# Head 0's row maxima through a scaled unit matrix, and a reordered prologue, in a bucketed-attention plus two-MoE kernel

## The chip, the cores and the metric

The kernel runs on one core of a Trainium2 chip. The metric is the device time of one execution in microseconds (us), the median of several runs. The engines are TensorE (PE in the profile; PEld is its weight load), VectorE (DVE), ScalarE (ACT), GpSimd (POOL) and SyncE (SP), which here only issues transfers. A q behind a name (SPq, ACTq) marks the instructions of an engine's sequencer, transfers above all. Each engine executes its own instructions in the order in which the program gives them.

## What is computed

Attention over 16 heads (batch 2 x 8), 768 positions, head size 64, in which a query sees only the keys of its own hash bucket, followed by two feed-forward layers (left out below, the change doesn't touch them):

```
q_bits = (einsum('bhsd,dk->bhsk', q, proj) > 0);  k_bits likewise      # 6 bits
mask   = q_bucket[..., :, None] == k_bucket[..., None, :]
scores = where(mask, q @ k^T / 8, -1e9)
attn   = exp(scores - max(scores)) ;  attn /= sum(attn) + 1e-9
out    = attn @ v                    # then moe(out), then moe2(...)
```

A row without any key in its bucket gets the plain mean of v.

## The kernel before

The heads go two at a time: a pair p holds heads 2p and 2p+1, on 64 partitions each. For a pair, `split_k`, `split_q` and `low_q` cut k and q into a rounded high part and a rest (`kH`, `kL`, `qH`, `qL`, in the fp32r format). For pair 0 VectorE makes the rests, for pair 1 GpSimd does, from values that ScalarE rounds or scales first. `bits` multiplies them with the projection (`prH`, `prL`, made from `pr` in `setup`) in six matmuls for each half of 384 positions, and a comparison on VectorE turns the sums into plus or minus one half (`bits_cmp` for head 0, `bits_bt` into the tile `bt` for the others, which `bits_out` copies by DMA into rows 64 to 75 of the head's tiles).

Each head h has a tile `KA` and a tile `QA` (in the trace both are called T, with a buffer number in the order listing: T_86 and T_91 are head 0, T_87 and T_92 head 1, and so on): rows 0 to 63 hold the high part, rows 64 to 75 the bits. `KB` and `QB` hold what the rounding left. Rows 96 and 97 of `QA` hold the row's maximum in two parts, and the same rows of `KA` are -1, so that the score matmul subtracts the maximum itself.

The work of a head:

- `max_unit(h, qt)`, six of them: for 128 queries, two matmuls (line 614) against all keys, and two VectorE reductions (line 618) to the maximum. Three PSUM buffers ("m") are shared by these and by the bit products.
- `max_fin` and `max_out`: the maxima (`mq`) are transposed on TensorE (line 634), split in two on VectorE (lines 637 and 638, tile `mr`) with a flag for rows without keys (`mf`, line 643), and copied by two DMAs into rows 96 and 97 of `QA`, by a third into `FL`. For head 0 this is done for each half of the queries.
- `scores(h, hf, i)`, six units s = 6h + 3hf + i: for 256 keys by 384 queries, two matmuls of 128 rows (KB, QB) and two of 98 rows (KA, QA), line 664. Then `Exp` on ScalarE twice (`E`, line 668, and rounded to fp16, `ph`, line 671), and on GpSimd the rest `pl` (line 686). Two PSUM buffers ("s") hold the scores; the prologue's bit products of pair 0 use the same two.
- `pv(h, hf, q)`: 20 matmuls (lines 698 to 704) with `ph`, `pl`, the flags and v, six units behind the scores (LAG = 6).

The order is written out by hand. `prologue()` loads pair 0, makes head 0's bits and maxima and, between the maxima, filler matmuls (`warm`, line 742) that write nothing that is used. Then a loop over the units s issues `pv(s-6)`, `scores(s)`, the maxima of later heads, and the tasks that tables put at unit s: `at(s, ...)` before, `po(s, ...)` at the end of the unit. Up to s = 7 the tasks stand behind the scores and the maxima of their unit. The maxima of head 1 are taken at s = 0 (one `max_unit`), 1 (one) and 2 (four). Constants such as E2 and E4 say at which s pair 1's row copies (`asm_k`, `asm_q`), `bits` and `bits_out` stand.

## Time and profile before

| | us |
|---|---|
| median of 3 runs | 680.44 |
| the three runs | 680.24, 680.44, 682.21 |
| the profiled execution | 680.07 |
| its span, first to last instruction | 678.3 |

| engine | busy, us | share of the span |
|---|---|---|
| PE | 662.5 | 98% |
| PEld | 611.0 | 90% |
| DVE | 510.2 | 75% |
| ACT | 432.5 | 64% |
| POOL | 338.2 | 50% |

Matmuls overlap and their ends are modelled, so a PE busy share of 98% says that it seldom had nothing in flight; it is the gaps, and what it did between them, that have to be read from the timeline. A timeline row gives the start, the length, the engine, the line, what was written and read, how many instructions the row merges, and, in brackets, how long the engine was idle before and what ended that. For a row of two matmuls the length covers both.

### The profile page before, as it was taken

The page shows a single profiled execution, that of the slowest core. Times are in us where ns is not written, and L with a number is a line of the kernel's source. Part 1 is how long each engine was busy: PE and PEld are TensorE (multiplying, and loading weights), DVE is VectorE, ACT ScalarE, POOL GpSimd, SP SyncE. Part 2 cuts the span into 40 slices and gives each one's busy share as a digit, 9 for nine tenths or more (in the row PEclk, how much of TensorE's full clock was granted, in tenths as well). Part 3 has the DMA queues.
Part 4 walks back from the last instruction along what each step waited for, and adds up shares of the span by engine and source line. Part 5 has one row for each costly group of instructions (what it writes and reads, how often), then busy time and mean ns, then how long its engine had stood idle before and what let it go on. Part 6 is the DMA issues. An engine that isn't in the chain of part 4 may idle for free.

```text
span 678.3 us, 13481 instructions
## 1 busy us (share of the span) xinstructions
PE 662.5 (98%) x5189; PEld 611.0 (90%) x5189; DVE 510.2 (75%) x978; ACT 432.5 (64%) x749; POOL 338.2 (50%) x280
## 2 busy tenths in 40 slices
PE   8999999999999999999999999999999999999998
PEld 7789998888898989999999999988989898989886
DVE  6798988999985557677768778754868787877664
ACT  6578788889888525465665657776656565565520
POOL 6688888999988240654542673122233131313100
PEclk9899999999999999999999999999999999999999
DMA  6656656767441000222114322010303121211005
GB/s 192 168 150 150 172 143 159 197 167 190 101 98 65 1 2 31 65 86 68 62 63 125 126 63 93 32 63 0 125 21 104 32 95 36 89 63 62 1 0 187
DMA packets 22527, 61.80 MB, mean 91 GB/s; under 512 B 3864, under 2 KB 4952, under 8 KB 22464
## 3 DMA queue, kind: packets, MB, share of 16 engines
q1 hardware_dynamic: 22032, 60.55, 31.3%
q8 instruction: 41, 0.67, 0.4%
q10 hardware_dynamic: 432, 0.40, 0.2%
q14 instruction: 22, 0.18, 0.1%
HBM read 38.87 MB, written 3.15 MB: 62 GB/s over the span
## 4 chain that ended last, share of the span: by engine, by line
PE 63%; DVE 6%; ACT 2%; issue 1%; POOLq 0%; DVEq 0%; ACTq 0%
PE c L1210 16%; PE m L1210 11%; PE x L1538 10%; PE m L1538 9%; PE c L147 4%; PE m L307 3%; PE m L1453 2%; PE s L664 2%; PE c L1453 2%; PE x L1210 1%; PE x L698 1%; DVE xF L1161 1%; PE x L699 1%; PE x L700 1%; DVE mx L618 1%
## 5 line engine op out<-in xcount | busy, mean ns | idle before, releaser
L686 POOL TENSOR_TENSOR pl<-E,ph 128x768 f16<-128x768 f32 x85 | 152.4, 1807 | 30.7 <-ACT ph L671 17.1
L618 DVE TENSOR_REDUCE mx<-m 128x1 f32<-128x384 f32 x192 | 96.7, 546 | 13.1 <-PE m L614 12.1
L668 ACT ACTIVATE E<-s 128x768 f32<-128x768 f32 x96 | 78.0, 813 | 38.5 <-PE s L664 31.5
L671 ACT ACTIVATE ph<-s 128x768 f16<-128x768 f32 x85 | 68.9, 811 | 0.0
L698 PEld LDWEIGHTS <-ph 128*128 128x128 f16 x576 | 53.7, 97 | 16.3 <-issue 10.2
L698 PE MATMUL x<-VV,ph 128*128 128x65 f16 x576 | 64.2, 195 | 2.8 <-DVE xo L718 1.8
L699 PE MATMUL x<-VV,ph 128*128 128x65 f16 x576 | 63.8, 195 | 0.0
L700 PE MATMUL x<-VV,pl 128*128 128x65 f16 x576 | 63.3, 192 | 0.0
L664 PE MATMUL s<-QB,KB 128*128 128x384 f32 x192 | 57.0, 378 | 0.0
L614 PE MATMUL m<-T,T 76*128 76x384 f32 x192 | 54.0, 354 | 2.7 <-DVE mx L618 1.5
L699 PEld LDWEIGHTS <-ph 128*128 128x128 f16 x576 | 54.3, 98 | 0.7 <-issue 0.6
L700 PEld LDWEIGHTS <-pl 128*128 128x128 f16 x576 | 54.5, 99 | 0.0
L664 PE MATMUL s<-T,T 98*128 98x384 f32 x192 | 49.6, 339 | 0.2 <-DMA T<-mr 0.2
L1006 POOL TENSOR_TENSOR hF<-hF 128x256 f32<-128x256 f32 x8 | 6.9, 859 | 75.5 <-DVE hF L965 75.5
L614 PEld LDWEIGHTS m<-T,T 76*128 76x128 f32 x192 | 35.2, 189 | 8.3 <-DVE mx L618 5.5
L961 DVE SCALAR_TENSOR_TENSOR wy<-wy,wr 128x512 int32<-128x512 int32 x32 | 23.0, 718 | 22.0 <-ACT wr L956 22.0
L1556 DVE TENSOR_TENSOR xF<-x,xF 128x512 f32<-128x512 f32 (+1 forms) x43 | 29.4, 684 | 11.6 <-PE x L1538 11.5
L1094 POOL TENSOR_TENSOR hF<-hF 128x256 f32<-128x256 f32 x6 | 6.5, 1091 | 62.7 <-DVE hF L1048 62.7
L984 POOL TENSOR_TENSOR wl<-wy,wh 128x512 fp32r<-128x512 f32 x10 | 13.0, 1298 | 46.4 <-ACT wh L982 46.4
L664 PEld LDWEIGHTS s<-T,T 98*128 98x128 f32 x192 | 35.2, 190 | 0.5 <-DMA T<-mr 0.5
L984 POOL TENSOR_TENSOR wol<-wy,woh 128x512 fp32r<-128x512 f32 x6 | 8.4, 1393 | 50.9 <-ACT woh L982 50.9
L1556 DVE TENSOR_TENSOR xF<-m,xF 128x512 f32<-128x512 f32 (+1 forms) x42 | 28.5, 678 | 4.6 <-PE m L1538 4.6
(472 smaller groups left out, 2185.1 us busy)
## 6 DMA issues: line engine op xcount, KB each, us to landing
wraw<-in_wts_dram SPq DMA_DIRECT2D x56, 512.0 KB
xF<-in_vP_dram SPq DMA_DIRECT2D x8, 384.0 KB
KB<-kH SPq DMA_DIRECT2D x15, 192.0 KB
QB<-qL SPq DMA_DIRECT2D x15, 192.0 KB
T<-kH SPq DMA_DIRECT2D x15, 192.0 KB
T<-qH SPq DMA_DIRECT2D x15, 192.0 KB
KB<-kL SPq DMA_DIRECT2D x15, 192.0 KB
QB<-qH SPq DMA_DIRECT2D x15, 192.0 KB
```

The lines of the kernel that those rows point to most:

```text
L614: pe.matmul(u[:, 0:HF], QA[h % NA][0:76, qt * 128:qt * 128 + 128], KA[h % NA][0:76, hsl(hf)], start=True, stop=True,)
L618: dve.tensor_reduce(out=mx[h][:, qt, hf:hf + 1], in_=u[:, 0:HF], axis=AX.X, op=ALU.max)
L664: pe.matmul(u[:, k, 0:HF], a[0:n, c], b[0:n, hsl(hf)], start=n == 128, stop=n < 128)
L668: act.activation(out=e, in_=u[:, :, 0:HF], func=AF.Exp, scale=BIG)
L671: act.activation(out=ph.rearrange("p (a b) -> p a b", a=2), in_=u[:, :, 0:HF], func=AF.Exp, scale=BIG,)
L686: eng.tensor_tensor(out=pl, in0=e, in1=ph, op=ALU.subtract)
L698: pe.matmul(o, ph[:, c], vv[:, 0:65], start=kt == 0, stop=False)
L699: pe.matmul(o, ph[:, c], vv[:, 65:130], start=False, stop=False)
L700: pe.matmul(o, pl[:, c], vv[:, 0:65], start=False, stop=False)
L1210: pe.matmul(u, l[:, s], r[i], start=first and i + j == 0, stop=i == 1 and j == 2, skip_group_check=not first,)
L1538: pe.matmul(u[:, 0:c1 - c0], (h, l, h)[k], (oh, oh, ol)[k][:, c0:c1], start=j == k == 0, stop=j == 1 and k == 2,)
L1556: dve.tensor_tensor(out=o, in0=u[:, 0:c1 - c0], in1=o, op=ALU.add)
```

## The change

Six edits, all of which act before head 1's scores:

- `load_qk(0)`: the projection `pr` is the first transfer on ScalarE's queue; before, it stood behind the first half of q.
- `prologue`: the row copies of head 0 (`own_rows`) stand behind the splits of both halves, and the four filler matmuls behind each half's bit products go (WARM 4 to 0).
- `bits_bt` of head 1 moves from ahead of the first `max_unit` to ahead of the fourth (B0 0 to 3).
- Head 0's maxima are no longer transposed and copied into `QA`. `max_diag(hf)` makes, for each half, the negated maxima, split in two (`nm`, `nh`, `nl`), and multiplies the unit matrix by them, column scale by column scale: three VectorE operations into `xh0[0]`, three ScalarE operations into `xl0[0]`. `scores` of head 0 then adds them with four more matmuls a unit, with a matrix of ones (`xh0[1]`) as weights; its second pair of matmuls reads 76 rows rather than 98.
- `max_flag(hf)` transposes the maxima for the flag alone, at s = 0 and s = 2.
- The split of pair 1 leaves the prologue for the end of unit 0, and its row copies and bit products stand at unit 1 rather than 0.

```
-B0 = 0
-F0 = 2
+B0 = 3
-WARM = (9, 4, 3, 1)
+WARM = (9, 0, 3, 1)
-E2 = (0, 0, 2)
+E2 = (1, 1, 2)
-E4 = ((0, 0), (2, 4), (3, 7))
+E4 = ((1, 1), (2, 4), (3, 7))
...
+            st["one"] = xh0[1][:, 0:128]
+            pool.memset(f32(st["one"]), 1.0)
...
+                act.dma_start(out=pr, in_=projT)
                 for c in (hsl(0), hsl(1)):
                     sp.dma_start(out=kr[:, c], in_=kT[p][:, c])
                     act.dma_start(out=qr[:, c], in_=qT[p][:, c])
-                    if c.start == 0:
-                        act.dma_start(out=pr, in_=projT)
...
+        def max_diag(hf):
+            n = a2.tile([128, 3], F32, name="nm")
+            dve.tensor_scalar(
+                out=n, in0=st["mq", 0][:, 3 * hf:3 * hf + 3], scalar1=-1.0, scalar2=0.5,
+                op0=ALU.mult, op1=ALU.min,
+            )
+            nh = a2.tile([128, 3], F32R, name="nh")
+            dve.tensor_copy(out=nh, in_=n)
+            nl = a2.tile([128, 3], F32, name="nl")
+            dve.tensor_tensor(out=nl, in0=n, in1=f32(nh), op=ALU.subtract)
+            d = [x[0][:, hsl(hf)] for x in (xh0, xl0)]
+            for b in range(3):
+                c = slice(128 * b, 128 * b + 128)
+                dve.tensor_scalar(
+                    out=d[0][:, c], in0=ident, scalar1=f32(nh)[:, b:b + 1], scalar2=None,
+                    op0=ALU.mult,
+                )
+                act.activation(
+                    out=d[1][:, c], in_=ident, func=AF.Identity, scale=nl[:, b:b + 1]
+                )
+            st["D", hf] = d
+
+        def max_flag(hf):
+            u = unit()
+            pe.transpose(u[0:3, 0:128], st["mq", 0][:, 3 * hf:3 * hf + 3], ident)
+            g = a2.tile([6, 128], F16, name="mf")[0:3]
+            dve.tensor_scalar(out=g, in0=u[0:3, 0:128], scalar1=-0.5, scalar2=None, op0=ALU.is_lt)
+            sp.dma_start(out=FL[0][0:1, hsl(hf)], in_=g)
...
-            for a, b, n in ((KB[h], QB[h], 128), (KA[h % NA], QA[h % NA], 98)):
+            for a, b, n in ((KB[h], QB[h], 128), (KA[h % NA], QA[h % NA], 98 if h else 76)):
...
+            for j in range(0 if h else 2):
+                for k in range(2):
+                    pe.matmul(
+                        u[:, k, 0:HF], st["one"], st["D", hf][j], start=False, stop=j == 1
+                    )
...
                 low_q(0, c)
+            for c in (hsl(0), hsl(1)):
                 own_rows(c)
...
-            split_k(1, slice(0, S), True)
-            split_q(1, slice(0, S), True)
-            low_q(1, slice(0, S))
...
                 warm(WARM[2] if qt < 3 else WARM[3])
-                if qt == F0:
-                    max_fin(0, 0)
-                    max_out(0, 0)
+                if qt % 3 == 2:
+                    max_diag(qt // 3)
...
+            if p == 1:
+                po(0, split_k, 1, slice(0, S), True)
+                po(0, split_q, 1, slice(0, S), True)
+                po(0, low_q, 1, slice(0, S))
...
-                po(E3[0], max_fin, 0, 1)
-                po(E3[1], max_out, 0, 1)
+                for i in range(2):
+                    po(E3[i], max_flag, i)
```

How the order moves, at three places. Line numbers of the changed kernel differ (scores 694 and 699, `Exp` 703 and 706, bit products 146, filler 777).

VectorE, from the comparison for head 1's bits (`bt`) to head 0's last maxima, before:

```order
L513 TENSOR_SCALAR bt<-s,pr 128x384 x2
L618 TENSOR_REDUCE mx<-m 128x1 x6
L625 TENSOR_REDUCE mq<-mx 128x3
L637 TENSOR_SCALAR mr<-m 3x128
L638 SCALAR_TENSOR_TENSOR mr<-m,mr 3x128
L643 TENSOR_SCALAR mf<-m 3x128
```

and after, from the first of head 0's reductions:

```order
L618 TENSOR_REDUCE mx<-m 128x1 x6
L625 TENSOR_REDUCE mq<-mx 128x3
L649 TENSOR_SCALAR nm<-mq 128x3
L654 CAST nh<-nm 128x3
L656 TENSOR_TENSOR nl<-nm,nh 128x3
L660 TENSOR_SCALAR xh_97<-ident,nh 128x128 x3
L513 TENSOR_SCALAR bt<-s,pr 128x384 x2
```

The `bt` comparisons moved behind the first half's maxima, and six new operations took the place of three; in both kernels six more reductions follow, and after those, in the changed one, the six operations again.

ScalarE, from the last of the constants (T_95) to the second score unit, before:

```order
L410 ACTIVATE T_95<-pr 32x768
L442 ACTIVATE kH<-kr 128x768
L457 ACTIVATE qH<-qr 128x768
L463 ACTIVATE qr<-qr 128x768
L668 ACTIVATE E<-s 128x768
```

and after (xl_101 is the tile `xl0[0]`):

```order
L411 ACTIVATE T_95<-pr 32x768
L664 ACTIVATE xl_101<-ident,nl 128x128 x6
L703 ACTIVATE E<-s 128x768
L706 ACTIVATE ph<-s 128x768
L442 ACTIVATE kH<-kr 128x768
L457 ACTIVATE qH<-qr 128x768
L463 ACTIVATE qr<-qr 128x768
```

The six scalings of both halves now stand ahead of the first `Exp`, and the three split operations of pair 1 between the first unit's `Exp` and the second's.

TensorE, from the first score unit to pair 1's bit products, before (head 1's first maxima between them):

```order
L664 MATMUL s<-QB,KB 128x384 x2
L664 MATMUL s<-T_91,T_86 128x384 x2
L614 MATMUL m<-T_87,T_92 128x384 x2
L147 MATMUL m<-kH,prH 128x384
L147 MATMUL m<-qH,prH 128x384
```

and after, from the second score unit on:

```order
L694 MATMUL s<-QB,KB 128x384 x2
L694 MATMUL s<-T_91,T_86 128x384 x2
L699 MATMUL s<-xh_97,xh_98 128x384 x2
L699 MATMUL s<-xl_101,xh_98 128x384 x2
L614 MATMUL m<-T_87,T_92 128x384 x2
L543 MATMUL m<-vs_s,ones 128x1
L146 MATMUL m<-kH,prH 128x384
L146 MATMUL m<-qH,prH 128x384
```

The twelve bit products (two of them shown) now stand between the second and the third score unit rather than between the first and the second, and a score unit has eight matmuls rather than four.

## Rows read from the trace of the kernel before

**Rows 1.** Busy time and granted clock in three stretches, columns as the first line says

```profile
core 0: us, PE busy (x) PEld busy (x) DVE busy (x) ACT busy (x) POOL busy (x), PEclk, DMA share, GB/s
27.00:31.00 4.00, 3.98 (x15) 3.38 (x15) 2.60 (x7) 1.62 (x2) 2.27 (x2) 0.57 0.77 163
36.00:50.00 14.00, 13.54 (x173) 12.20 (x172) 12.83 (x35) 10.48 (x14) 11.10 (x7) 1.00 0.66 159
100.00:245.00 145.00, 140.14 (x1895) 126.59 (x1894) 122.29 (x282) 115.28 (x170) 120.34 (x76) 1.00 0.47 119
```

**Rows 2.** Timeline of the prologue (start us, length us), splits and bits of pair 0

```profile
0.99 4.21 PE L742 MATMUL x<-ones 128*128 128x128 f32 x18 [0.99 <-POOL ones L383]
...
4.30 0.51 ACT L457 ACTIVATE qH<-qr 128x384 fp32r<-128x384 f32 x1
...
4.89 0.17 DVE L379 CAST prH<-pr 64x24 fp32r<-64x24 f32 x1 [4.89 <-DMA pr<-in_projT_dram]
...
5.67 0.66 PE L147 MATMUL s<-kH,prH 128*128 128x384 f32 x1 [0.48 <-ACT T L479]
5.77 0.56 DVE L443 TENSOR_TENSOR kL<-kr,kH 128x384 fp32r<-128x384 f32 x1
...
6.13 0.52 PE L147 MATMUL s<-qH,prH 128*128 128x384 f32 x1
...
6.45 0.52 PE L147 MATMUL s<-kH,prL 128*128 128x384 f32 x1
...
7.40 1.05 PE L742 MATMUL x<-ones 128*128 128x128 f32 x8
...
9.17 0.33 PE L147 MATMUL s<-qL,prH 128*128 128x384 f32 x1
...
9.54 1.25 DVE L513 TENSOR_SCALAR T<-s,pr 12x384 fp32r<-12x384 f32 x2 [0.52 <-PE s L147]
```

**Rows 3.** Timeline from head 0's maxima to the first Exp

```profile
15.68 1.45 SPq L142 DMA_DIRECT2D T<-mr  x2
...
16.09 2.86 DVE L618 TENSOR_REDUCE mx<-m 128x1 f32<-128x384 f32 x6
...
18.78 0.30 PEld L664 LDWEIGHTS s<-T,T 98*128 98x128 f32 x2 [0.47 <-DMA T<-mr]
...
19.44 0.81 ACT L668 ACTIVATE E<-s 128x768 f32<-128x768 f32 x1 [0.99 <-PE s L664]
```

**Rows 4.** Timeline, the split of pair 1 on ScalarE and GpSimd

```profile
15.83 0.84 ACT L442 ACTIVATE kH<-kr 128x768 fp32r<-128x768 f32 x1 [2.57 <-PE m L614]
...
16.75 1.83 POOL L443 TENSOR_TENSOR kL<-kr,kH 128x768 fp32r<-128x768 f32 x1 [1.86 <-ACT kH L442]
...
17.60 0.84 ACT L463 ACTIVATE qr<-qr 128x768 f32<-128x768 f32 x1
```

**Rows 5.** Timeline of the first units, from the first ph to the fourth scores

```profile
20.14 0.80 ACT L671 ACTIVATE ph<-s 128x768 f16<-128x768 f32 x1
...
22.70 0.60 PE L664 MATMUL s<-QB,KB 128*128 128x384 f32 x2
...
24.45 0.60 PE L664 MATMUL s<-QB,KB 128*128 128x384 f32 x2
...
25.00 0.14 DVE L549 TENSOR_SCALAR vs_t<-m 128x1 f32<-128x1 f32 x1
...
25.63 3.80 DVE L618 TENSOR_REDUCE mx<-m 128x1 f32<-128x384 f32 x8
...
30.14 0.93 PE L664 MATMUL s<-QB,KB 128*128 128x384 f32 x2
```

**Rows 6.** Timeline, SyncE's transfers to head 1's maxima, and head 1's first scores

```profile
25.92 0.66 SPq L651 DMA_DIRECT2D FL<-mf  x1
...
32.87 1.52 SPq L142 DMA_DIRECT2D T<-mr  x2
...
37.40 0.52 PE L664 MATMUL s<-T,T 98*128 98x384 f32 x2
```

More of the change, by code (lines that the diff above doesn't have):

```diff
@@ L664, in scores @@
                     pe.matmul(
-                        u[:, k, 0:HF], a[0:n, c], b[0:n, hsl(hf)], start=n == 128, stop=n < 128
+                        u[:, k, 0:HF], a[0:n, c], b[0:n, hsl(hf)], start=n == 128, stop=n == 98
+                    )
[3 more added lines that the diff above has]
+                        u[:, k, 0:HF], st["one"], st["D", hf][j], start=False, stop=j == 1
                     )
```

## The prediction, made before the changed kernel was run

> **What bounds the kernel now.** I read three views. The busy time by stretch comes first: from 100 to 245 us, most of the attention, TensorE is busy 140.14 of 145.00 us, and from 36 to 50 us 13.54 of 14.00 [rows 1]. From about 36 us on TensorE is therefore the bound, at a fixed amount of work, and a later start of that stage moves the end by the same amount, but for the idle time that it can give back: at most 0.46 + 4.86 = 5.3 us. Second, the timeline of the first 37 us, in which the stage is filled. Its marks are the first `Exp` at 19.44 us [rows 3], the second and third score units at 22.70 and 24.45, the eight reductions for head 1's maxima from 25.63, the fourth unit at 30.14 [rows 5], and head 1's first scores, which need its maxima, at 37.40 [rows 6]. Third, the timeline of SyncE's queue: the flags of head 0 leave at 25.92, head 1's maxima at 32.87, 6.95 us later, with eight other transfers between them, back to back [rows 6]. I compare the changed kernel with the last mark, 37.40 us.
>
> **The start of the prologue.** VectorE's first work waits for the projection until 4.89 us [rows 2]. Loaded first, it comes before the first rounded k and q are there; VectorE's four set-up operations then lie beside that load. TensorE, though, can't start the bits before its nine fillers end, 0.99 + 4.21 = 5.20 us, against 5.67 now: 0.47 us. The eight filler rows between the halves (four matmuls, two rows each) take 1.05 us [rows 2], of which 0.8 lie on the path to the second half's products, since these pipeline behind them. Those now end at 9.17 + 0.33 = 9.50, so then at 8.2. Head 0's four comparisons, 1.25 us for two [rows 2], end at 10.79 now; VectorE then takes them one after the other from about 7.2, so they end at 9.7. The moved `own_rows` lie on ScalarE, which has no one waiting for them before 9 us; cost nothing. The memset of the ones (128 x 128) on GpSimd lies beside its own wait; cost nothing.
>
> **Head 0's maxima.** From 9.7 us on VectorE is the chain. Six reductions take 2.86 [rows 3]. The maximum of the pairs and the three operations on 128 x 3 cost about 0.19 each (0.14 plus the hand-over, [rows 5], whose 128 x 1 operation is nearest): 0.76. The three products with the unit matrix aren't in the trace; they lie between 0.14 (128 x 1) and 0.56 (128 x 384, [rows 2]); I take 0.2, a third of the larger: 0.6. Then the two `bt` comparisons, 1.2 as those of head 0, six more reductions 2.86, and 0.76 again. Sum: 9.7 + 2.86 + 0.76 + 0.6 + 1.2 + 2.86 + 0.76 = 18.7. ScalarE's six scalings stand ahead of the first `Exp` in its queue, those of the second half too, though the first unit doesn't need these. They are unseen as well: between 0.14 and 0.51 (128 x 384, [rows 2]), I take 0.2 each, three after 18.7. First `Exp`: 19.4 us. Now it is at 19.44. The copies of the maxima by DMA, issued from 15.68, held up TensorE by 0.47 us at 18.78 [rows 3]; that wait is gone, and the new chain over VectorE and ScalarE is late in its place, at the same time. **Gain up to here: none.**
>
> **The split of pair 1.** ScalarE did it from 15.83 in idle time, and GpSimd followed from 16.75 [rows 4]. Now it stands behind the first unit's two `Exp`. From 19.4: `ph` starts 0.70 later [rows 3, 5] and takes 0.80, so `kH` starts at 20.9; the three splits start 0.885 apart (15.83 to 17.60 in two steps, [rows 4]) and end at 23.5. The second unit's `Exp` is queued behind them; it came late before as well, behind the bits, so little changes there. GpSimd's `kL` runs from 21.8 for 1.83 [rows 4], and `qL`, as long, ends at 25.5. TensorE has twelve bit products between the second unit's maxima and the third unit. It reaches them at about 22 (scores at 16.9 after the ninth reduction, second unit by 21.7), does four or five and **waits for `qL` until 25.5**. Behind the waiting product stand seven matmuls with it, then the third unit, then head 1's eight maxima, and VectorE waits for these.
>
> **The clock.** TensorE's granted clock, 1.00 elsewhere, averages 0.57 from 27 to 31 us [rows 1], that is, it is at 1.2 GHz for most of it: there TensorE did eight products at the pace of the reductions. Matmuls of 384 columns stand 0.18 apart at full clock (0.52 for a pair, 0.33 for one, [rows 6, 2]) and 0.32 apart at the lower (6.13 to 6.45, [rows 2]). In the new wait of about 3.5 us TensorE does less than in that stretch, so I take the lower clock when it resumes, until the bits are done, and the full one after. The Trainium skill (TensorE: Matmul & The Clock Gate, section on HAM oscillation) speaks against this change in the same way: bursts of matmuls with waits between them each begin at half clock. By that rule the time is the first case's below, without it that of the first rival; no row shows a wait of this length.
>
> First case: the bits end at 25.5 + 7 x 0.32 = 27.7, the third unit, eight matmuls at 0.18, at 29.2, the first product 0.35 later is with VectorE: the eight reductions begin at 29.55 instead of 25.63, **+3.9**.
>
> **The extra matmuls.** 24 in all, four in each of six units, 24 x 0.18 = 4.3 us at full clock. Those of the first three units are in the times above. Twelve remain, 2.15 us, between the eight reductions and head 1's scores, where TensorE is dense; a transposition more costs 0.2. Head 1's scores by TensorE's own work: 37.40 + 3.9 + 2.15 + 0.2 = 43.65, **+6.25**.
>
> **The flags.** The second flag now leaves VectorE only behind the eight reductions: 29.55 + 3.80 + 0.5 for the last maximum and the flag's comparison = 33.9, against 25.92. SyncE waits there, and the 6.95 us of transfers queue behind: head 1's maxima leave at 40.85. From issue to use the earlier copies took 18.78 - 15.68 = 3.1 [rows 3]; they land at 43.95, **+6.55**. This comes last, just.
>
> Sum: +6.5 us at the mark. The profiled execution took 680.07 us (its span 678.3 and 1.77 around it), so 686.6; the median of the runs shown is 0.37 higher, 680.44, and I forecast against that: **686.9 us**.
>
> **The rivals.**
>
> Full clock. TensorE doesn't slow down in the wait. Seven products take 1.25 instead of 2.25, and the reductions start at 28.55; flags, and with them head 1's maxima, come 1.0 earlier: +5.5, 686.0. For it: in the other stretches of rows 1 the clock is at 1.00. Against it: none of them holds such a wait, and 27 to 31, with a milder one, is low.
>
> Given back later. The shift at the mark is right, but VectorE, GpSimd and SyncE are not delayed as much as TensorE afterwards, and TensorE's waits for them shrink. At most 5.3 us are there [rows 1]; many are gaps of a tenth of a microsecond or two, which no lead removes. I price half: 6.5 - 2.65 = +3.85, 684.3; all of it, 681.6. Against it: SyncE and VectorE are delayed as well.
>
> Not slower: the bits find their operands. Were `qL` there when TensorE arrives, the third unit would end at 25.5 (22.0 + 12 x 0.18 + 8 x 0.18), the reductions would begin at 25.9, +0.3, and the fillers and the fourth unit, now at the lower clock (1.7 us lost from 27 to 31, [rows 1]), might run at the full one: 0.3 + 2.15 + 0.2 - 1.7 = +0.95, 681.4. It decides at `qL`'s end: 23.5 us, two earlier than I have it, so a first `Exp` by 17.4. For that the comparisons would have to end at 7.7, when the second half's bits aren't yet done. A little less still, and the kernel is faster. This is also the case in which the change does what its first half says; I think that the gain of about 1 us at 9.7 us is real and is used up by the new operations before the first `Exp`.
>
> **How the numbers follow.** Lower clock in the wait 0.45 (686.9), full clock 0.27 (686.0), given back later 0.20 (684.3), operands in time 0.08 (681.4). The lower bound: full clock and half the idle time given back, 683.2. The upper: ScalarE's scalings at 0.51 each put the first `Exp` 0.9 later, and a lower clock through the whole third unit adds 8 x 0.14 = 1.1: 688.9. Range **683.0 to 689.0**; left out are the last rival, the end of the third and what I haven't seen above, together under 2 in 10. A measurement of this kernel can tell about 0.3%, 2.0 us: slower means above 682.5. Slower 0.88; within 0.3% 0.09 (most of the last rival, and the full give-back); faster 0.03.
>
> **What would show it.** In the changed profile: VectorE's first operation before 4.4 us; head 0's comparisons done at 9.7; the first `Exp` at 19.4, led by ScalarE's scalings; ScalarE's `kH` for pair 1 at 20.9, GpSimd's `qL` ending at 25.5; TensorE idle before the sixth bit product of pair 1, at a granted clock of 0.50 afterwards; the eight reductions from 29.5; SyncE's second flag at 33.9; head 1's scores waiting for the copy of its maxima at about 44. I am wrong if the first `Exp` comes before 17.5 us, if the bits don't wait for GpSimd, or if head 1's scores shift by 6 us and the end doesn't.

## The result and the profile after

| | before | after |
|---|---|---|
| median, us (4 runs each) | 681.26 | 689.71 |
| lowest and highest | 680.24, 682.21 | 689.47, 691.09 |
| the profiled execution | 680.07 | 689.47 |
| its span | 678.3 | 687.7 |

The changed kernel takes 1.0125 times as long (95% interval 1.0111 to 1.0139): slower, as forecast, but by 8.45 us between the medians and 9.4 between the profiled executions, where I had 6.5. 689.71 lies above the range's upper end of 689.0.

Where the time went is read from the start of each unit's first `Exp`, compared unit by unit with the kernel before (units are counted from 0): 1.83 us later at unit 0, 4.76 at unit 2, 7.28 at unit 5 and 7.26 at unit 7, then 9.61 at unit 8, and 9.2 to 9.3 from unit 11 to the last of the attention, unit 95. All the loss lies in the first 53 us, in steps, and only 0.3 us of it is given back behind unit 8.

The windows of the changed kernel, in the columns of [rows 1]:

```profile
core 0: us, PE busy (x) PEld busy (x) DVE busy (x) ACT busy (x) POOL busy (x), PEclk, DMA share, GB/s
13.00:16.00 3.00, 0.11 (x1) 0.00 (x0) 2.93 (x9) 1.84 (x5) 1.11 (x2) 1.00 0.96 351
16.00:23.00 7.00, 6.51 (x24) 6.32 (x25) 5.51 (x16) 2.72 (x6) 0.00 (x0) 0.53 0.09 17
23.00:27.00 4.00, 3.55 (x21) 3.23 (x20) 1.68 (x4) 3.54 (x5) 3.41 (x2) 0.96 0.33 85
33.00:37.00 4.00, 3.98 (x17) 3.72 (x18) 1.54 (x5) 0.42 (x1) 3.20 (x2) 0.57 0.11 25
38.00:50.00 12.00, 11.64 (x126) 10.69 (x124) 9.94 (x25) 6.56 (x10) 6.59 (x4) 1.00 0.79 210
110.00:254.00 144.00, 139.10 (x1889) 125.66 (x1888) 121.30 (x280) 115.03 (x169) 119.35 (x76) 1.00 0.46 118
```

From 13 to 16 us TensorE does almost nothing (0.11 of 3.00) while VectorE is busy for 2.93; then TensorE works 16 to 23 us at a granted clock of 0.53 on average, that is at 1.2 GHz for nearly all of it. The kernel before has 1.00 there. The stage in which TensorE is the bound looks as before: 139.10 of 144 us.

The timeline of the stretch in which head 0's maxima are made and the first units start (the second `xl` and `E` are ScalarE's, start and length in us):

```profile
12.00 2.11 POOL L402 MEMSET FL<- 128x768 f16 x3
12.03 0.55 DVE L618 TENSOR_REDUCE mx<-m 128x1 f32<-128x384 f32 x1
12.80 0.63 DVE L649 TENSOR_SCALAR nm<-mq 128x3 f32<-128x3 f32 x1
13.47 0.66 DVE L654 CAST nh<-nm 128x3 fp32r<-128x3 f32 x1
14.16 0.16 DVE L656 TENSOR_TENSOR nl<-nm,nh 128x3 f32<-128x3 f32 x1
14.83 1.14 DVE L513 TENSOR_SCALAR bt<-s,pr 128x384 fp32r<-128x384 f32 x2
16.49 0.69 PE L614 MATMUL m<-T,T 76*128 76x384 f32 x1 [3.37 <-DVE mx L618]
19.21 0.17 DVE L649 TENSOR_SCALAR nm<-mq 128x3 f32<-128x3 f32 x1
19.41 0.17 DVE L654 CAST nh<-nm 128x3 fp32r<-128x3 f32 x1
19.82 0.99 ACT L664 ACTIVATE xl<-ident,nl 128x128 fp32r<-128x128 f32 x3 [4.47 <-DVE nl L656]
21.27 0.81 ACT L703 ACTIVATE E<-s 128x768 f32<-128x768 f32 x1 [0.47 <-PE s L699]
22.67 0.84 ACT L442 ACTIVATE kH<-kr 128x768 fp32r<-128x768 f32 x1
25.38 1.83 POOL L464 TENSOR_TENSOR qL<-qr,qH 128x768 fp32r<-128x768 f32 x1
25.95 0.42 PE L146 MATMUL m<-kH,prH 128*128 128x384 f32 x1 [0.45 <-DVE mx L618]
27.27 0.45 PE L146 MATMUL m<-qL,prH 128*128 128x384 f32 x1 [0.20 <-POOL qL L464]
30.38 3.81 DVE L618 TENSOR_REDUCE mx<-m 128x1 f32<-128x384 f32 x8 [0.33 <-PE m L614]
44.67 0.52 PE L694 MATMUL s<-T,T 98*128 98x384 f32 x2
```

The same `nm` and `nh` take 0.63 and 0.66 us in the first half and 0.17 each in the second. The six `xl` cost 0.33 each, between my ends. The first `Exp` [rows 3] comes at 21.27 instead of 19.44, the eight reductions [rows 5] at 30.38 instead of 25.63, head 1's first scores with the maxima [rows 6] at 44.67 instead of 37.40.

And SyncE's transfers with the one ScalarE operation that waits for them:

```profile
23.72 0.69 SPq L674 DMA_DIRECT2D FL<-mf  x1
34.61 0.69 SPq L674 DMA_DIRECT2D FL<-mf  x1
41.54 1.52 SPq L141 DMA_DIRECT2D T<-mr  x2
45.02 0.59 SPq L141 DMA_DIRECT2D KB<-kH  x1
50.75 0.85 ACT L442 ACTIVATE kH<-kr 128x768 fp32r<-128x768 f32 x1 [2.76 <-DMA KB<-kH]
52.23 0.79 ACT L703 ACTIVATE E<-s 128x768 f32<-128x768 f32 x1
```

Between 34.61 and 41.54 stand the eight other transfers of [rows 6], back to back as before. New is the last wait: the rounding of k for pair 2 overwrites the tile that `KB<-kH` reads, that copy was issued at 45.02 (36.35 in the kernel before), and ScalarE stands still for 2.76 us with the `Exp` of unit 8 queued behind. It is the step from 7.26 to 9.61. The same two rows of the kernel before:

```profile
36.35 0.59 SPq L142 DMA_DIRECT2D KB<-kH  x1
41.03 0.85 ACT L442 ACTIVATE kH<-kr 128x768 fp32r<-128x768 f32 x1 [0.30 <-DMA KB<-kH]
```

The wait grew by 2.46 us. Of these, 1.41 are the queue's: the copy left 8.67 us later, while ScalarE itself was 7.26 late. The other 1.05 are the copy's own: the wait for it ended 5.73 us after its issue, against 4.68 before. Why it took longer is open.

### The profile page after: what moved, and what is told of

The parts are those of the page before. It is cut to its first block, busy times and chain, and to the rows that moved or that the text cites. A ratio compares the mean times of both kernels' runs of the same rounds, so it can differ in the third digit from the quotient of the medians.

```text
span 687.7 us, 13503 instructions
## 1 busy us (share of the span) xinstructions
PE 668.4 (97%) x5197; PEld 616.4 (90%) x5197; DVE 514.2 (75%) x986; ACT 434.1 (63%) x755; POOL 338.5 (49%) x281
## 4 chain that ended last, share of the span: by engine, by line
PE 61%; DVE 6%; ACT 2%; issue 1%; DMA 1%; POOLq 0%; DVEq 0%; ACTq 0%; SPq 0%
PE c L1246 16%; PE m L1246 10%; PE x L1574 9%; PE m L1574 9%; PE c L146 4%; PE m L306 3%; PE m L1489 2%; PE s L694 2%; PE c L1489 2%; PE x L1246 1%; DMA wraw<-in_wts_dram 1%; PE x L733 1%; DVE xF L1197 1%; PE x L734 1%; PE x L735 1%
## 5 line engine op out<-in xcount | busy, mean ns | idle before, releaser
L694 PE MATMUL s<-T,T 98*128 98x384 f32 (+1 forms) x192 | 50.1, 342 | 0.0
L694 PEld LDWEIGHTS s<-T,T 98*128 98x128 f32 (+1 forms) x192 | 35.8, 192 | 0.0
```

The costliest lines, as they stand in the source:

```text
L694: pe.matmul(u[:, k, 0:HF], a[0:n, c], b[0:n, hsl(hf)], start=n == 128, stop=n == 98)
```

## The experiments

Times of one kernel scatter by 1.5 to 6 us, so that medians of few runs settle little; each verdict below rests on the places in the trace, and the ratio is given beside it. All are against the kernel before.

| kernel | first Exp | eight reductions from | later than before at unit 0 / 7 / 8 / 95 | ratio, 95% |
|---|---|---|---|---|
| before | 19.44 | 25.63 | 0 | 1 |
| after | 21.27 | 30.38 | 1.83 / 7.26 / 9.61 / 9.27 | 1.0125 (1.0111 to 1.0139) |
| a2_after (unedited) | 20.99 | 30.11 | 1.55 / 6.97 / 9.07 / 11.17 | 1.0115 (1.0077 to 1.0153) |
| b2_before (unedited) | 19.74 | 26.14 | 0.30 / 1.72 / 1.70 / 1.80 | one run, 681.84 us |
| e1b_flags | 21.00 | 30.11 | 1.56 / 7.37 / 8.26 / 8.55 | 1.0091 (1.0061 to 1.0120) |
| e12_flagq | 20.76 | 31.39 | 1.32 / 8.19 / 8.18 / 8.71 | 1.0087 (1.0067 to 1.0106) |
| e2_split | 21.06 | 28.30 | 1.62 / 5.04 / 7.66 / 8.80 | 1.0099 (1.0077 to 1.0121) |
| e3_fill | 20.20 | 29.25 | 0.76 / 6.02 / 7.65 / 8.47 | 1.0101 (1.0078 to 1.0123) |
| e4_split_fill | 21.72 | 27.94 | 2.28 / 4.85 / 6.11 / 6.24 | 1.0059 (1.0037 to 1.0081) |
| e5_fl | 21.13 | 30.22 | 1.69 / 8.09 / 9.27 / 9.41 | 1.0117 (1.0094 to 1.0139) |
| e13_fl2 | 19.90 | 30.52 | 0.46 / 7.33 / 10.42 / 11.57 | 1.0136 (1.0121 to 1.0151) |
| e14_comb | 21.88 | 28.09 | 2.44 / 3.38 / 3.37 / 3.63 | 1.0080 (1.0060 to 1.0101) |
| e11_nodiag | 18.36 | 27.20 | -1.08 / 2.22 / 4.91 / 4.50 | 1.0050 (1.0033 to 1.0067) |
| e7_pro | 19.05 | 27.16 | -0.39 / 1.68 / 1.68 / 1.74 | 0.9979 (0.9964 to 0.9994) |
| e16_fill | 18.23 | 24.54 | -1.21 / -0.81 / -0.82 / -0.76 | 0.9989 (0.9975 to 1.0003) |
| e17_fill2 | 18.17 | 24.40 | -1.27 / 0.57 / 1.16 / 1.26 | 1.0008 (0.9990 to 1.0027) |
| e18_fill1 | 18.36 | 25.60 | -1.08 / 2.16 / 3.61 / 4.12 | 1.0000 (0.9981 to 1.0019) |

A part of these differences is scatter. after, a2_after and e12_flagq give TensorE, VectorE and ScalarE the same instructions up to unit 3, yet head 0's first reduction begins at 9.62, 9.34 and 9.74 us, the granted clock is back at 1.00 from about 23 us in the first two and from about 20.5 in the third, and pair 1's bit products begin at 25.95, 25.68 and 24.41.

### The flags on SyncE's queue

My theory after the result: the flags hold up SyncE's queue, and the copies behind them the units from 8 on. The first edit was run twice, since the profiled execution of the first (e1_flags) took 1000.8 us and can't be compared; its other runs have the ratio 1.0085 (1.0056 to 1.0115):

```
-E3 = (0, 2)
+E3 = (3, 4)
```

> The changed kernel with head 0's two flags sent later: their transposition, comparison and copy stand at units 3 and 4 instead of 0 and 2. In the changed kernel the shift against the kernel before is 7.26 us at the Exp of unit 7 and 9.61 at unit 8, and ScalarE waits 2.76 us there for a copy of kH. Queue theory: SyncE stood still for the flags (6.0 and 3.4 us) and all copies behind came late; without that ScalarE's wait falls under 0.6 us, unit 8's shift equals unit 7's, and the time is 2.0 us less, about 687.5. Rival: the copy lands late because TensorE and ScalarE were late themselves, the queue is not the cause; then the wait stays and the time is 689.5.

> The changed kernel with head 0's two flags taken at units 3 and 4 instead of 0 and 2 (E3 = (3, 4)), so that SyncE's queue no longer waits for the flag's comparison behind the first units' maxima. The earlier kernel with this edit (0.997 of its time scaled by nothing, 688.56 median) left no usable trace; this one is for the trace. Queue theory: KB<-kH of pair 1 leaves before 41 us instead of 45.02, ScalarE's kH of pair 2 waits under 0.6 us for it instead of 2.76, the lag behind the kernel before is the same at unit 8 as at unit 7 (7.3), and the end comes 2.0 us earlier than in the changed kernel: 687.6. Rival (the jump at unit 8 is made by GpSimd or ScalarE, the copy only happens to end last): kH of pair 2 waits as long for something else, unit 8 lags by 9.2 to 9.6 as before, 689.5 within 0.5.

Inconclusive: the step at unit 8 shrank from 2.35 to 0.89, the wait of `kH` to 1.29 us. But the flags, made later, held the queue at 39.06 and 44.23, and `KB<-kH` left at 45.63, not before 41:

```profile
45.63 0.59 SPq L141 DMA_DIRECT2D KB<-kH  x1
49.39 0.85 ACT L442 ACTIVATE kH<-kr 128x768 fp32r<-128x768 f32 x1 [1.29 <-DMA KB<-kH]
```

So the copy left 0.61 later than in the changed kernel and was still done 1.36 earlier, 3.76 us after its issue: the moment of issue isn't all that counts. The next kernel keeps the flags where they are made and puts off their transfers alone (the flag's tile is called `mg` in it):

```
-            sp.dma_start(out=FL[0][0:1, hsl(hf)], in_=g)
+            st["mg", hf] = g
+
+        def flag_out(hf):
+            sp.dma_start(out=FL[0][0:1, hsl(hf)], in_=st["mg", hf])
...
                     po(E3[i], max_flag, i)
+                    po(3, flag_out, i)
```

> The changed kernel with head 0's two flags still made at units 0 and 2, but their transfers on SyncE's queue put off to the end of unit 3, behind the row copies and loads that stood behind the second flag. Queue theory (SyncE, held by the flags, sends head 1's maxima and the row copies behind them late, and ScalarE's kH of pair 2 waits for these): KB<-kL, kH and so on leave from 31 us instead of 35.4, head 1's maxima at 39 instead of 41.5, KB<-kH of unit 7 at 42.5 to 43.5 instead of 45.0, kH of pair 2 waits under 1 us instead of 2.76, and the lag behind the kernel before is the same at unit 8 as at unit 7, about 7.3; end 2.0 earlier, 687.5. Rival (the copies land when the DMA engines have moved what is queued, whatever the order): kH of pair 2 waits over 2 us again, the lag jumps to 9 at unit 8, 689.5.

Its transfers and the operation of ScalarE:

```profile
31.83 0.59 SPq L141 DMA_DIRECT2D KB<-kH  x1
35.69 1.53 SPq L677 DMA_DIRECT2D FL<-mg  x2
39.85 1.51 SPq L141 DMA_DIRECT2D T<-mr  x2
43.32 0.59 SPq L141 DMA_DIRECT2D KB<-kH  x1
48.82 0.83 ACT L442 ACTIVATE kH<-kr 128x768 fp32r<-128x768 f32 x1
```

`kH` has no wait left, and the shift is 8.19 at unit 7, 8.18 at unit 8 and 8.20 at unit 11. The step of 2 us goes with the flags' place in SyncE's queue. Of the 2.76 us of waiting, 1.70 are the copy's earlier issue and 0.93 ScalarE's own later arrival. (That the shift stands at 8.2 and not 7.3 goes with TensorE's clock, 0.50 from 28 to 30 us, where the changed kernel has 1.00.) At the end this execution is 0.56 us ahead of the changed kernel's and not 2.0; the ratios, 1.0087 and 1.0125, have intervals that don't meet.

### The split of pair 1, and TensorE's clock

Fillers at the fourth maxima (e3, the first piece), the split back in the prologue (e2, the two others), and both (e4):

```
-                warm(WARM[2] if qt < 3 else WARM[3])
+                warm(14 if qt == 3 else WARM[2] if qt < 3 else WARM[3])
...
+                if qt == 2:
+                    split_k(1, slice(0, S), True)
+                    split_q(1, slice(0, S), True)
+                    low_q(1, slice(0, S))
...
-            if p == 1:
-                po(0, split_k, 1, slice(0, S), True)
-                po(0, split_q, 1, slice(0, S), True)
-                po(0, low_q, 1, slice(0, S))
```

> The changed kernel with pair 1's split on ScalarE and GpSimd back in the prologue, right behind the first half's maxima; all else as changed. The prediction's step (the bits' wait for GpSimd is what holds the third unit): head 1's eight reductions begin 2.4 us or more earlier than 30.4, time about 687 or less. Two-path theory: TensorE, at the lower clock from 16.5 to 23.2 us, reaches the bits only at 25.9 and waits 0.5 us for GpSimd, so the split alone gives back 0.5 us, the reductions begin at 29.8, time about 689.0.

> The changed kernel with 13 more filler matmuls behind the fourth maximum of head 0, which fill the 3.6 us in which TensorE waits for VectorE; nothing else. Two-path theory: the granted clock stays at 1.00 from 16 to 23 us, but the first Exp can't come before ScalarE's scalings end (20.8), and pair 1's split behind it holds the bits: reductions begin at 29.9 instead of 30.4, time about 689.1. Rival, the clock alone is the loss: matmuls of 5.9 us at half clock return 2.9 us, time about 686.6.

> Both of the two edits before: pair 1's split back in the prologue, and the fillers in TensorE's wait. Two-path theory: each edit alone leaves the other path as the bound, both together free the start: eight reductions from about 26.7, time 3.7 us less, about 685.8, more than the two gains added. Rival, the gains add up: about 688.6 by the first theory's single values.

A row of e2, TensorE's wait at head 1's scores:

```profile
42.37 0.59 PE L694 MATMUL s<-T,T 98*128 98x384 f32 x2 [1.21 <-DMA T<-mr]
```

And one of e3, its wait in the bit products:

```profile
26.14 0.44 PE L146 MATMUL m<-qL,prH 128*128 128x384 f32 x1 [1.32 <-POOL qL L464]
```

In e2 the reductions come 2.1 us earlier than in the changed kernel. About 0.5 of this is the wait for `qL`, which is gone, as the two-path theory had it. The rest is that TensorE reaches the bits at 24.34 instead of 25.95, its clock being back at 1.00 from 20 us rather than 23:

```profile
20.00:22.00 2.00, 2.00 (x16) 1.91 (x15) 1.85 (x7) 1.83 (x5) 0.00 (x0) 1.00 0.04 8
```

e12, which has the changed kernel's split, reached them as early (24.41), so that e2 doesn't show these 1.6 us to be the split's. The end comes only 0.5 earlier: head 1's scores now wait for the copy of the maxima, which the same queue sends at 39.45, `kH` of pair 2 waits 3.03, and a stretch at 0.50 from 54 to 57 us adds 1.6 at unit 11. In e3 the clock stays at 1.00 up to 31 us. The first `Exp` comes 1.1 us earlier, of which 0.36 lie ahead of the edit (head 0's first reduction begins at 9.26 instead of 9.62), and TensorE then waits for `qL`, which the first `Exp` gates. So there are two paths to the third unit that are nearly level, TensorE's at half clock and the one over ScalarE's queue to GpSimd: where TensorE comes early (e3, e12), it waits 1.2 to 1.3 us for `qL`. That only both edits together free the start is not shown, since at the reductions e2 alone brings 2.1 and both bring 2.4. At the end both together bring 3.0, where the two alone bring 0.5 and 0.8.

### VectorE beside GpSimd

`nm` and `nh` took 0.63 and 0.66 us while GpSimd set the three FL tiles to zero. That is a matter of order: the second memset ends at 13.41 (12.68 + 0.73), `nm` at 13.43; the third at 14.11, `nh` at 14.13. VectorE's cast stands still until GpSimd's instruction has ended. The reduction at 12.03, also beside a memset, took its usual 0.55. The Trainium skill (SBUF — State Buffer, section Who interferes with whom) says that casts and tensor_scalar between SBUF operands can take a port pair that GpSimd shares, whole, for an instruction, and that reductions never do; the trace agrees on both. Two edits. In e5 the memsets stand earlier, in the prologue:

```
-            for t in FL:
-                pool.memset(t, 0.0)
...
+            for t in FL:
+                pool.memset(t, 0.0)
```

In e13 those of FL[1] and FL[2] are put off behind pair 1's split:

```
-            for t in FL:
-                pool.memset(t, 0.0)
+            pool.memset(FL[0], 0.0)
...
+            if p == 1:
+                po(0, lambda: [pool.memset(t, 0.0) for t in FL[1:]])
```

> The changed kernel with the memsets of the tiles FL moved on GpSimd to where it is idle, at 4 to 6.5 us, away from 12 to 14.1 us where they lie beside VectorE's nm and nh of the first half. Contention theory (VectorE's small operations are stretched while GpSimd works): nm and nh of the first half take 0.17 us each instead of 0.63 and 0.66, the first bt comparison and all behind it come 0.95 earlier, first Exp 20.3 instead of 21.27, eight reductions at 29.4, end 0.9 earlier: 688.8. First-use theory (an operation of a form that VectorE has not done before is slow the first time): nm and nh still take 0.6 us each, first Exp 21.3, 689.5 or no change.

> The changed kernel with the memsets of FL[1] and FL[2] moved behind GpSimd's qL of pair 1 (only FL[0] is left at 12.0 us, ending before VectorE's nm). Lock theory (a cast or scaling of VectorE from SBUF to SBUF stands still until GpSimd's memset has ended): nm and nh of the first half take 0.17 us each, all behind them comes 0.95 us earlier, first Exp at 20.3, eight reductions at 29.4; end 0.9 earlier, 688.6, if the late memsets hold up nobody. Rival (the memsets cost the same wherever they lie): VectorE or GpSimd lose 1 us behind unit 0 and the end does not move, 689.5.

VectorE in e5, with the memsets from 3.98 to 6.08:

```profile
4.07 0.18 DVE L379 TENSOR_TENSOR prL<-pr,prH 64x24 fp32r<-64x24 f32 x1
4.25 1.85 DVE L378 CAST prH<-pr 64x24 fp32r<-64x24 f32 x1
14.12 0.17 DVE L647 TENSOR_SCALAR nm<-mq 128x3 f32<-128x3 f32 x1
14.32 0.17 DVE L652 CAST nh<-nm 128x3 fp32r<-128x3 f32 x1
```

First use is out: the operations take 0.17. But the stall only moved: now the cast of the projection stands for 1.85 us, everything behind it is 1.3 later, and nothing is gained. In e13 neither is stalled (both 0.17), and the first `Exp` comes 1.37 us earlier than in the changed kernel, 1.14 if both are counted from head 0's first reduction. The gain is gone by unit 2: the clock is 0.50 from 27 to 29 us, in the bit products, and the reductions start at 30.52. Behind them the queue costs 3.1 us at unit 8 (`kH` of pair 2 waits 3.49), and a stretch at 0.50 from 58 us on takes the shift to 11.57. The cause of the stretched operations is confirmed, the 0.9 at the end was a miss.

### All mends at once, and the maxima's old way

e14 has the edits of e4, e12 and e13 together. e11 keeps all of the change but the maxima: these are transposed and copied as in the kernel before, without the 24 matmuls. The edit of e11 at its main place:

```
-                if qt % 3 == 2:
-                    max_diag(qt // 3)
+                if qt == 2:
+                    max_fin(0, 0)
+                    max_out(0, 0)
```

> All four mends together in the changed kernel: split of pair 1 in the prologue, fillers at the fourth maxima that hold the clock, the flags' transfers put off to unit 3, the memsets of FL[1] and FL[2] put off. The two first together gave a lag of 4.85 at unit 7 and 6.25 at the end. If the queue and the lock are what was left: no jump at unit 8, a lag of 4 to 5 at the end, 684.5. The 24 matmuls with the ones are still in it (4.3 us at 0.18 each), so below 683 would say that they cost less than their own time. Rival (each mend only lets the next wait come up): lag 6 at the end, 686.4.

> The changed kernel with head 0's maxima again transposed, split and copied by DMA into rows 96 and 97, as in the kernel before: no scaled unit matrices, no matmuls with the ones, 98 rows again; the other edits (projection first, no filler, row copies behind the splits, bt moved, split and bits of pair 1 at units 0 and 1) stay. If the price of the changed kernel is the maxima's new way (24 matmuls at 0.18 = 4.3 us, of which all but those that TensorE's waits cover reach the end, and a first Exp 1.9 later than forecast): first Exp at 18.8, qL of pair 1 ending at 24.7, eight reductions at 26.9, and 683.8, that is 5.7 under the changed kernel. If the price is the later split of pair 1 (its qL gates the third unit whatever came before): reductions at 28 or later and 686 to 688.

e14's profiled execution has a clock of 1.00 throughout, no wait of `kH`, and no step at unit 8. What is left is 3.4 us. e16 below, which has the prologue's edits without the maxima's new way, also at full clock up to 26 us, is 0.81 ahead. The difference, 4.19, is near 24 matmuls at 0.18 = 4.3, but it doesn't show their price: the two kernels differ in more, their first `Exp` by 3.65, and e16 is at 0.50 from 27 to 30 us where e14 is not. The four runs of e14 lie between 683.3 and 689.2, and the profiled one is the fastest, so the median gain is smaller than the trace's. VectorE's standstill beside GpSimd is there too, in the second half, where `nm` waits for GpSimd's `qL` and two memsets (17.35 to 20.53):

```profile
17.88 2.68 DVE L648 TENSOR_SCALAR nm<-mq 128x3 f32<-128x3 f32 x1
```

e11 halves the loss: of 9.27 us at the end 4.50 stay. The first `Exp` (18.36) and the reductions (27.20) come where the first theory had them, but the end doesn't: pair 1's later bits send `T<-bt` at 26.68 instead of 22.62 and with it the whole queue. TensorE waits for head 1's maxima at unit 6, ScalarE for a row copy ahead of unit 8:

```profile
39.55 0.59 PE L692 MATMUL s<-T,T 98*128 98x384 f32 x2 [1.72 <-DMA T<-mr]
46.04 0.85 ACT L440 ACTIVATE kH<-kr 128x768 fp32r<-128x768 f32 x1 [3.09 <-DMA QB<-qL]
```

Neither reading I had written was whole: up to unit 5 the kernel is only 0.27 us late, and the later split then costs through SyncE, not through the reductions.

### The prologue's edits alone

e7 is the kernel before with the projection first, the row copies behind both splits, and no fillers behind the bits; e16 adds fillers between head 0's maxima; e17 and e18 add more at unit 2. The pieces below are e7 (beside the two moves, which are those of the change), e16, and e17 (1 instead of 2 in e18).

```
-WARM = (9, 4, 3, 1)
+WARM = (9, 0, 3, 1)
...
-                warm(WARM[2] if qt < 3 else WARM[3])
+                warm((5, 3, 5, 2, 2, 1)[qt])
...
+                warm(2 if s == 2 else 0)
```

> The kernel before with three edits of the changed one alone: the projection first on ScalarE's queue, the row copies behind both halves' splits, no fillers behind the bit products. From the changed kernel's trace these bring head 0's comparisons from 10.79 to 9.6 us. Theory (they are a gain that the other edits use up): the six maxima and with them the first Exp come 0.8 to 1.2 us earlier than at 19.44, the eight reductions at 24.6 to 24.9, the end 0.8 to 1.0 earlier than the kernel before. Rival (the copies of the maxima on SyncE, or the split of pair 1, end last and give nothing back): first Exp at 19.2 to 19.5, no difference.

> The kernel before with the projection first, the row copies behind both splits and no fillers behind the bits (as e7_pro), and more fillers between head 0's maxima (5, 3, 5, 2, 2, 1 instead of 3, 3, 3, 1, 1, 1), where e7_pro's TensorE idled and its clock was 0.50 from 17 to 23 us. Theory: the clock stays at 1.00 to 25 us, second Exp at 22.8 instead of 25.20, eight reductions at 24.7, and the end 1.0 to 2.0 earlier than e7_pro's profiled execution; median 679.5 to 680.5 against 682.2 of the kernel before. Rival (the fillers delay the maxima, and the clock falls anyway): no earlier than e7_pro, 681 to 682.

> e16_fill with two filler calls (four rows) behind each of head 1's maxima at unit 2, where TensorE goes at the pace of the eight reductions and its clock falls to 0.50. If the fall goes with the idle time: the clock stays at 1.00 to 36 us, the fourth Exp comes 1.0 earlier than in e16_fill (29.7 instead of 30.70), the lag at the end is -1.5 to -1.8 instead of -0.8, and the median 0.3 to 0.4% under the kernel before. If the fillers stand in the way of the maxima (0.26 each at full clock, 0.5 at half): reductions 1 us longer, lag 0 or above, 681.5.

> As e17_fill2 with one filler call instead of two. If one is enough to hold the clock: as e17_fill2 or 0.2 better. If not: 0.50 from 27 us as in e16_fill, lag -0.8, 680.7.

e7 is 0.2% faster (12 runs), the only kernel here that is faster by more than its interval. Its profiled execution is not one that shows it: it ran at 0.50 from 17 to 23 us. e16's holds the clock there, its first `Exp` comes 1.21 us earlier and 0.8 of that reaches the end; its interval just includes no change. The 1 us that the prediction saw in the prologue is there at the first `Exp` where the clock holds. e17 and e18 failed: the fillers came to stand in one row behind all eight maxima, not between them, the clock had fallen at 26 us already, and at half clock they only delayed the fourth unit.

### Two kernels once more

> The changed kernel once more, unedited, for a second profile. If its half clock is fixed by what TensorE does: 0.50 again from 16 or 17 to 23 us, the same lags behind the kernel before (1.8 at the first unit, 7.3 at unit 7, 9.2 at the end), 689.5. If it differs from execution to execution: the fall starts or ends elsewhere, by 1 us or more, and the lag at unit 7 lies between 6.0 and 8.5 with it; the jump at unit 8, which the flags on SyncE's queue make, is there in either case.

> The kernel before once more, unedited, for a second profile. The first was one of its fastest executions (680.07 of runs from 680.2 to 684.7), at a clock of 1.00 up to 27 us. If the spread of the runs is the clock's: an execution of 681.5 or more shows 0.50 in a stretch in which the first has 1.00, and lies behind by the time lost there; an execution near 680 shows the clock of the first.

The granted clock is the third number from the right in a row of these windows. The kernel before in its first profile, one row that was not shown:

```profile
31.00:35.00 4.00, 3.98 (x35) 3.57 (x34) 3.33 (x8) 3.16 (x5) 2.81 (x3) 1.00 0.77 250
```

And in the second profile, b2_before:

```profile
25.00:27.00 2.00, 1.68 (x9) 1.29 (x9) 1.90 (x8) 1.76 (x3) 1.22 (x1) 1.00 0.13 23
27.00:31.00 4.00, 3.98 (x14) 3.16 (x14) 3.11 (x8) 2.12 (x3) 2.19 (x3) 0.56 0.65 138
31.00:35.00 4.00, 4.00 (x17) 3.73 (x16) 2.33 (x6) 1.52 (x3) 2.45 (x2) 0.59 0.92 273
```

The clock falls at the same place, in the reductions [rows 1], but is back at 1.00 by 31 us in the one and averages 0.59 from 31 to 35 in the other, and this execution is 1.7 us behind from unit 5 to the end. The changed kernel repeats its pattern (0.50 from 17 to 22 us, `kH` of pair 2 waiting 2.50, 9.07 at unit 8). The half clock at 17 us is thus the changed kernel's own, but not that of the maxima's new way alone. e7 and e11, which lack it, are at 0.50 from 17 to 23 and from 16 to 22 us, as this row of e7 shows:

```profile
17.00:22.00 5.00, 4.83 (x16) 4.35 (x15) 2.17 (x6) 2.23 (x3) 3.83 (x3) 0.50 0.82 204
```

They share with it the faster prologue without the fillers behind the bits, and more fillers between the maxima hold the clock with the new way (e3) and without it (e16). a2_after's further 2.5 us, near 150 us, I had not expected: TensorE waits there for the copy of a head's maxima, issued at 144.32 while the DMA engines are 90% and more busy, and runs at 0.50 afterwards:

```profile
150.46 0.58 PE L694 MATMUL s<-T,T 98*128 98x384 f32 x2 [0.93 <-DMA T<-mr]
```

Why in this execution and not in the other is open.

## Why the prediction was right in sign and short in size

- **The start: right.** VectorE's first operation is at 3.55 (I had before 4.4), the last comparison ends at 9.59 (9.7). In e7 and e16 head 0's first reduction begins 1.2 to 1.4 us earlier than in the kernel before.
- **First Exp: three terms too small.** 19.4 forecast, 21.27 measured. The operations on 128 x 3 were priced at 0.19 each by a row that reads PSUM while GpSimd is idle [rows 5]; two of them stood behind memsets, 0.95 more, and e13 shows it. The three scalings ahead of the `Exp` took 0.99 and not 0.6. The `Exp` then waited 0.47 for scores that TensorE made at half clock: I had counted VectorE's chain of 3 us and more ahead of the second half's maxima, but not that TensorE stands idle beside it, and that its clock falls. Of these 1.9 us, 0.83 are left at the reductions and 0.7 at the mark.
- **The split of pair 1: the mechanism right, its term shifted with the first Exp.** `kH` at 22.67 (20.9), `qL` ending at 27.21 (25.5), both 1.7 to 1.8 late.
- **The clock at the wait for qL: wrong in place.** TensorE, itself late, reached the bits at 25.95, waited there for half a microsecond rather than 3.5, and did them at full clock, as in the first rival. The half clock lies in 16 to 23 us, one wait earlier. The two errors partly cancel: the reductions came at 30.38, 0.83 after the forecast. The spacing of 0.32 at the lower clock was taken from 6.13 to 6.45 us, where the profile gives the granted clock as 1.00; in the changed kernel's stretch at 0.50 it is 0.32 as well (pairs of score matmuls start at 19.11, 19.75 and 20.39).
- **Twelve matmuls between reductions and mark: right.** 2.35 forecast; 7.28 at unit 5 less 4.75 at the reductions is 2.53.
- **The flags: right up to the mark.** The flag left at 34.61 (33.9), head 1's maxima at 41.54 (40.85), and TensorE used them at 44.67 (43.95), with no wait shown. In e2, e5 and e11, where TensorE did wait for this copy, it was there 2.9 to 3.0 us after its issue; by that, an estimate, it came here at 44.4 to 44.6, nearly level with TensorE's own work. At the mark the shift is 7.27, 0.7 above the forecast.
- **From the mark to the end: the step that failed.** I took the mark for the last place where the shift can grow ("a later start of that stage moves the end by the same amount") and put everything behind it at nothing. The queue that was 8.7 us late went on to send `KB<-kH` 8.67 us late, to a reader, ScalarE's `kH` of pair 2, that had no slack: it waited 0.30 for this copy in the kernel before. The wait became 2.76, and the shift 9.61 at unit 8 and 9.27 at the end. I had listed who waits for the maxima, not who waits for what is queued behind them. These 2.0 us are most of the miss of 2.8. That they go with the flags is shown by e12 and e14, where the step is gone, and by e1b, where it shrinks; why the copy was also slower to land is open.
- **Given back later: fell.** The shift never shrinks by more than 0.7 us from one unit to the next and ends at 9.27. **Operands in time** fell as well.
- **The base.** I summed on the execution of 680.07, whose clock came back early; the other profiled one (b2) pays 1.8 us more, which narrows the difference of the medians.

The cause in short: the step of 2.0 us behind the flags is shown. The 24 matmuls are 4.3 us of the 9.3 by their own length, an estimate from 0.18 each; of the twelve behind the reductions the trace shows 2.53 with a transposition, but no run takes out the matmuls alone. e11, without all of the maxima's new way, ends 4.8 us earlier. The rest is the idle TensorE with its half clock, VectorE's standstill beside GpSimd, and the split behind the first `Exp`, less 1 us gained at the start. These overlap, so that they have no sum of parts.

## What to carry to other kernels

When a wait is added to a queue, follow every transfer behind it to its reader, beyond the mark at which you compare, and give each the slack that its row shows. Before pricing a small VectorE operation, look at what GpSimd does in the same microsecond: the time moved with the memsets and left only when VectorE had nothing of that kind beside them. A chain that is moved from DMA to VectorE can leave TensorE idle, here for 3.4 us, and the price then includes the matmuls at half clock behind it. An edit worth 1 us is smaller than what one program differs by from execution to execution: compare several profiles before giving a shift to an edit.

## What the runs showed of the hardware

- VectorE's casts and scalings between SBUF tiles, 0.17 us alone, took up to 2.68 us when GpSimd was in a memset or a tensor_tensor, and ended within 0.03 us of it. A subtraction of two SBUF tiles, 0.16 alone, took 1.68 beside `qL` (e4, the row below), but 0.18 beside a memset (e5). The Trainium skill (SBUF — State Buffer, section Who interferes with whom) has this as well: two SBUF inputs contend with a GpSimd instruction that reads SBUF, not with one that only writes it.

```profile
19.11 1.68 DVE L656 TENSOR_TENSOR nl<-nm,nh 128x3 f32<-128x3 f32 x1
```

- The same program returns to full clock at different times after the same fall (the kernel before: by 31 us, or after 34). Its runs scatter from 680.2 to 685.4 us, of which this explains 1.7 in one pair of profiles. After the fall at 16 to 17 us it came back at about 23 us in two profiles of the changed kernel and at about 20.5 in e12, with nothing on TensorE edited up to there.
- The clock fell behind a stretch (13 to 16 us) in which TensorE waited for VectorE, and stayed at 1.00 up to 31 us when fillers stood in the gap (e3).
